# Second MoE layer on one core: raw weights given back earlier, converted weights stored later and in column parts, probability rows fetched one job earlier, and another order at the end

## The chip, the cores and the metric

The program runs on one NeuronCore of a Trainium2 chip. The metric is the device time of one execution in microseconds (us). TensorE is PE in the profile, VectorE is DVE, ScalarE is ACT, GpSimd is POOL; SyncE (SP) computes nothing here and issues the DMA transfers.

## The reference

Three layers follow one another on 2304 tokens of width 512, all in fp32: a causal decayed attention, a squared-ReLU layer with a hidden width of 2048, and a layer of four experts of hidden width 1024 that are weighted by probabilities and all added up.

```python
ret = scale * (q @ k.T) * Dmat;  x = ret @ v            # 4 batches, 8 heads, 576 x 64
h = x @ w_in;  g = max(h, 0) ** 2;  x = g @ w_out        # 512 -> 2048 -> 512
p = domain_probs / domain_probs.sum(-1)                  # 2304 x 4
for e in range(4):
    h = np.maximum(x @ w1[e], 0.0)                       # 512 -> 1024
    out += p[:, e:e+1] * (h @ w2[e])                     # 1024 -> 512
```

## The kernel before

**Precision.** PE multiplies in a rounded fp32 format. Each fp32 operand is therefore split into a high and a low part (`hi`, `lo`), and each product is three matmuls: hi·hi, hi·lo, lo·hi. The splitting is a copy on ACT (L130) and a subtraction on POOL (L131). A "matmul" below is one 128x128 weight tile against 512 columns; the usual step is six of them.

**Stages.** Attention takes the first 79 us of the span, the first layer (chunks c = 0 to 7 of its hidden width) runs to about 487 us, and the rest is the expert layer. That layer has 16 chunks, four to an expert, and passes over them twice: pass 1 (c = 8 to 23) serves the tokens of groups 0, 1 and 4, pass 2 (c = 24 to 39, from about 911 us) those of groups 2 and 3. Groups have 512 tokens, group 4 has 256.

**Seven products.** Two groups are treated together as a 2x2 block matrix, and its product with the 2x2 blocks of the weights is made by seven products instead of eight. For this the weights are needed as the four raw blocks (A11, A12, A21, A22; H11, H12, H21, H22) and as four sums of them (S1 to S4; for w2 t[0] to t[3]). In pass 1 the first multiplication of a chunk is `layer1_pair` (seven such products, ReLU and split in between), in pass 2 it is `first_layer`; the second multiplication in pass 1 is plain (`layer2_2`, which adds into `oacc`), in pass 2 it is `second_layer`, also seven products, which gathers into the four `sums`. `outputs` adds the last chunk, multiplies by a scale (`back`), and writes.

**Weights.** In pass 1 raw weights come by DMA into three buffers (`wraw`, `load_piece`); a chunk's w1 and w2 have two pieces each, and `load_piece()` asks for the next one as soon as one can be freed. `split_w1` and `split_w2` make the eight blocks (sums on DVE, L167 and L199; copies on ACT; subtractions on POOL), and `keep` stores the result to DRAM (L210), so that pass 2 only has to `fetch` it (L223). These functions are generators: every `yield` is a step, and `tick(pace)` runs `pace` steps of the queue `work` behind each group of matmuls. In pass 1 a chunk has 36 ticks at pace 3; conversion and storing want 26 steps of a chunk.

**Order.** Every engine works through its instructions in program order, and SP does so with the DMAs: an instruction that waits holds up all that stand behind it on its engine. So where a step stands in `work` decides what it can hold up. The list `jobs` gives the order of the multiplications; the last are pair(22), pair(23), group 4 of chunk 22, group 4 of chunk 23, and pair(24) of pass 2; the second multiplication of a job follows one job later. `probabilities()` (L771) broadcasts four rows of probabilities to all partitions, into the memory of the accumulators of groups 0 and 1; `first_layer` multiplies with them after its ReLU (L802).

**Pass 2.** Each of the seven products of chunk c is followed by one of the seven steps of `second_layer(c-1)` (L875 matmuls; sums on DVE, L885). Operands of that layer need further differences on POOL (L805), split again; four of these are put off into `later`. The first product of a chunk, A11, is copied from its bank by ACT (L811), and the fourth, A12, is accumulated in the same bank.

Of the kernel before, what the change touches and what calls it, by code (L numbers as in the profile page):

```python
# [28 lines left out]
BC = 256  # L29
# [4 lines left out]
def tile_kernel(ctx, tc, qT, kT, kn, vn, v4d, mask, qdec, kdec, wd, w, probs, probs2, out, outT):  # L34
# [104 lines left out]
    def split_w1(c):  # L139

        hi = wp.tile([128, 8 * BC], F32R, name="w1hi")
        lo = wp.tile([128, 8 * BC], F32R, name="w1lo")
        blk = [slice(BC * i, BC * (i + 1)) for i in range(8)]
        if c < NW1:

            w1s[c] = [t[:, :W1C].rearrange("p (f k m) -> p f k m", f=FT, k=KT) for t in (hi, lo)]
            for i in range(4):
                r = wraw.pop((c, i))
                yield from from_f64(r, hi[:, blk[i]], lo[:, blk[i]])
                load_piece()  # L150
# [12 lines left out]
        for i in (A11, S2, S3, A12, S1, A22, S4, A21):  # L163
            for _ in range(2 if todo else 0):
                yield
                o, x, y, op = todo.pop(0)
                v.tensor_tensor(out=o, in0=x, in1=y, op=op)  # L167
            yield
            split(src[i], hi[:, blk[i]], lo[:, blk[i]])
        load_piece()  # L170
        load_piece()

    def split_w2(c):

# [10 lines left out]
            return  # L185
        r = wraw.pop((c, 2)), wraw.pop((c, 3))
        a = [r[i // 2][:, BC * (i % 2) : BC * (i % 2 + 1)] for i in range(4)]
        for i in range(4):
            yield
            split(a[i], hi[:, blk[i]], lo[:, blk[i]])  # L190
        v = nc.vector
        t = [cvp.tile([128, BC], F32, name=n, bufs=2) for n in ("cv_m", "cv_d", "cv_m", "cv_d")]
        todo = [
            (t[0], a[H21], a[H22], ALU.add), (t[1], t[0], a[H11], ALU.subtract), (t[2], a[H21], a[H11], ALU.subtract),
            (t[3], a[H12], t[1], ALU.subtract),
        ]
        for i, (o, x, y, op) in enumerate(todo):
            yield
            v.tensor_tensor(out=o, in0=x, in1=y, op=op)  # L199
            yield  # L200
            split(o, hi[:, blk[4 + i]], lo[:, blk[4 + i]])
        load_piece()
        load_piece()

    def keep(f, c):

        yield
        for i, t in enumerate(w1t[c] if f is split_w1 else w2t[c]):
            d = dram.tile([128, 8 * BC], F32, name=f"kept{int(f is split_w2)}_{c}_{i}")
            nc.sync.dma_start(out=d, in_=f32(t))  # L210
            kept[f, c, i] = d

    def fetch(f, c):

        names = ("w2hi", "w2lo") if f is split_w2 else ("w1hi", "w1lo")
        parts = ((0, 3), (4, 8))
        if f is split_w2:
            parts = ((0, 1), (2, 8)) if c < NW - 1 else ((0, 4),)
        t = [wp.tile([128, 8 * BC], F32R, name=n) for n in names]
        for a, b in parts:  # L220
            for i in range(2):
                p = slice(BC * a, BC * b)
                nc.sync.dma_start(out=f32(t[i][:, p]), in_=kept[f, c - NW2, i][:, p])  # L223
# [19 lines left out]


    order = [(f, c) for c in range(NW) for f in (split_w1, split_w2)]
    splits = {}
    free = {(f, c) for f in (split_w1, split_w2) for c in range(2)}

    held = {(split_w2, NW1), (split_w1, NW1 + 1)}
# [1 line left out]
    def queue_weights(*place):  # L251
        free.update(place)
        while order and order[0] in free and order[0] not in held:
            f, c = order.pop(0)
            if c >= NW1 + NW2:
                fetch(f, c)
                continue
            splits[f, c] = f(c)
            work.append(splits[f, c])
            if c >= NW1:  # L260
                work.append(keep(f, c))


    def attention(a):
# [230 lines left out]
    with tc.manual_schedule():  # L495
# [428 lines left out]
        def outputs(c):  # L924
# [8 lines left out]
                nc.scalar.activation(out=t, in_=t, func=ACTF.Copy, scale=0.5)  # L933
                back.append(t)
            e1, e2, e3, e4 = totals()
            for a, b, op in ((e2, e1, ALU.add), (e3, e2, ALU.subtract), (e4, e3, ALU.subtract)):
                for d in range(2):
                    x, y = (a, b) if op == ALU.add else (b, a)
                    nc.gpsimd.tensor_tensor(out=a[d], in0=x[d], in1=y[d], op=op)
            for e, half, g, xs in (  # L940
                (e1, 0, 1, ("11", "21")), (e2, 0, 0, ("12", "22")), (e3, 1, 0, ("12", "22")), (e4, 1, 1, ("11", "21"))
            ):
# [43 lines left out]
        for i, job in enumerate(jobs):  # L986
# [2 lines left out]
            if c < NW1 + NW2:  # L989
                drain(splits[split_w1, c])  # L990

            pace[0] = 4 if i < 3 else 3 if c in (p, q) else 4 if c == z else 3 if c >= NW1 else 2
            if job == (NW1, (0, 1)):

                drain(sa[2])
# [38 lines left out]
            while i > 2 and len(pend) > 1:  # L1034
# [2 lines left out]
                layer2(done)  # L1037
                if j == last[done[0]]:
                    queue_weights((split_w2, done[0] + 2))
            if job == (z, (4,)):  # L1040
                probabilities()
            if job == (p, (3,)):
                rescale(0, s)
# [2 lines left out]
        sums += [yp.tile([128, 4, GT], F32, name=f"sums{i}", tag=f"acc{i}") for i in (2, 3)]  # L1046
        for c in range(NW1 + NW2 + 1, NW):
            f, t = first_layer(c), second_layer(c - 1)
            for _ in f:
                if later:  # L1050
                    later.pop(0)()
                next(t)
            queue_weights((split_w1, c + 2), (split_w2, c + 1))
        outputs(NW - 1)

# [71 lines left out]
```

## Time and profile before

| | |
|---|---|
| median of 3 runs | 1243.87 us (1243.79 to 1249.62) |
| the profiled execution's own time | 1243.94 us |
| its span, first to last instruction | 1242.0 us |
| PE busy | 1202.4 us (97%) |
| DVE busy | 897.5 us (72%) |
| POOL busy | 681.6 us (55%) |
| ACT busy | 435.3 us (35%) |
| mean granted PE clock | 0.994 |
| pass 1 of the expert layer | from about 480 to 911 us |
| pass 2 | from about 911 us to the end |

A busy PE does not say that nothing can be gained: what counts is where PE stands still, and what ended each such pause. A matmul that begins after a pause is shown with the idle time and the instruction that released it. After a long pause the granted clock can be below 1.00, and the matmuls behind it then take longer.

### The profile page before, as it was taken

Reading aid. Unit: us, or ns where it says so; the run is one execution under the profiler, and the core shown is the slowest. Engines: PE = TensorE matmul, PEld = TensorE weight load, DVE = VectorE, ACT = ScalarE, POOL = GpSimd, SP = SyncE. Lnnn points to the kernel's source line nnn. Section 1 sums busy time; section 2 is a strip of 40 time slices with the busy share of each in tenths; the row PEclk is TensorE's granted clock in tenths of the full one; section 3 lists DMA queues with packets and bytes.
Section 4 is the critical chain, followed back from the end, with each engine's and each line's share of the span. In section 5 each row is a group of like instructions: output and inputs, shape, how many; then the busy total and the mean of one; then the engine's idle time right before and its main releaser. Section 6 shows DMA issues by size and latency. Waiting matters only on the chain.

```text
span 1242.0 us, 18075 instructions
## 1 busy us (share of the span) xinstructions
PE 1202.4 (97%) x6470; PEld 1006.1 (81%) x6470; DVE 897.5 (72%) x1522; ACT 435.3 (35%) x1036; POOL 681.6 (55%) x695
## 2 busy tenths in 40 slices
PE   7999999999999999999999999999979999999997
PEld 6888888888888887778888878888768888888885
DVE  3777677777787688466777786767846877878777
ACT  4545433333333344533333433333402222222221
POOL 5646555545455435554553454533207777777776
PEclk9999999999999999999999999999989999999999
DMA  9921111111111002665455445555366465464551
GB/s 338 315 80 59 43 43 51 43 52 43 51 43 52 17 8 90 251 246 221 185 233 209 170 169 209 223 205 203 127 253 236 153 222 193 163 237 157 199 170 68
DMA packets 60989, 187.26 MB, mean 151 GB/s; under 512 B 7650, under 2 KB 12514, under 8 KB 52708
## 3 DMA queue, kind: packets, MB, share of 16 engines
q1 hardware_dynamic: 60388, 185.40, 40.9%
q8 instruction: 51, 0.84, 0.3%
q10 hardware_dynamic: 512, 0.70, 0.2%
q14 instruction: 38, 0.31, 0.1%
HBM read 114.23 MB, written 71.85 MB: 150 GB/s over the span
## 4 chain that ended last, share of the span: by engine, by line
PE 81%; DVE 9%; DMA 3%; ACT 2%; issue 2%; POOL 1%; SPq 0%; ACTq 0%; DVEq 0%; POOLq 0%
PE h L546 18%; PE o L741 14%; PE o L710 14%; PE h L792 11%; PE h L875 11%; PE h L580 10%; DMA wraw<-w 2%; DVE xl L669 1%; PE qk L347 1%; DVE y L637 1%; DMA k_n<-kn 1%; DMA rows<-rows 1%; PE xo L399 1%; DVE y L676 1%; DVE oacc L749 1%
## 5 line engine op out<-in xcount | busy, mean ns | idle before, releaser
L131 POOL TENSOR_TENSOR glo<-r,ghi 128x512 fp32r<-128x512 f32 (+1 forms) x80 | 96.9, 1212 | 153.6 <-ACT ghi L130 143.4
L546 PE MATMUL h<-xh,w1hi 128*128 128x512 f32 (+1 forms) x448 | 154.1, 344 | 0.8 <-DVE xl L434 0.8
L546 PE MATMUL h<-xl,w1hi 128*128 128x512 f32 (+1 forms) x448 | 154.0, 344 | 0.0
L546 PE MATMUL h<-xh,w1lo 128*128 128x512 f32 (+1 forms) x448 | 153.9, 344 | 0.0
L885 DVE TENSOR_TENSOR sums<-sums,h 128x512 f32<-128x512 f32 x202 | 128.5, 678 | 1.9 <-PE h L875 1.9
L741 PE MATMUL o<-w2hi,ghi 128*128 128x512 f32 x320 | 125.3, 392 | 3.1 <-DVE oacc L749 3.0
L741 PE MATMUL o<-w2hi,glo 128*128 128x512 f32 x320 | 125.0, 391 | 0.0
L741 PE MATMUL o<-w2lo,ghi 128*128 128x512 f32 x320 | 124.7, 390 | 0.0
L131 POOL TENSOR_TENSOR w2lo<-wraw,w2hi 128x256 fp32r<-128x256 f32 x64 | 52.2, 844 | 128.0 <-ACT w2hi L130 128.0
L710 PE MATMUL o<-glo,w2hi 128*128 128x512 f32 (+1 forms) x320 | 118.1, 369 | 1.0 <-POOL glo L131 1.0
L710 PE MATMUL o<-ghi,w2hi 128*128 128x512 f32 (+1 forms) x320 | 117.8, 368 | 0.0
L710 PE MATMUL o<-ghi,w2lo 128*128 128x512 f32 (+1 forms) x320 | 117.7, 368 | 0.0
L749 DVE SCALAR_TENSOR_TENSOR oacc<-o,pr,oacc 128x512 f32<-128x512 f32 x150 | 108.7, 743 | 5.8 <-PE o L741 5.7
L551 DVE TENSOR_TENSOR r<-r 128x512 f32<-128x512 f32 (+1 forms) x80 | 62.3, 779 | 65.5 <-ACT r L550 65.2
L580 PE MATMUL h<-xh,w1hi 128*128 128x512 f32 x224 | 88.6, 396 | 7.6 <-ACT r L593 3.9
L792 PE MATMUL h<-xh,w1hi 128*128 128x512 f32 x224 | 88.8, 397 | 6.9 <-DVE spare_xh L799 6.9
L546 PEld LDWEIGHTS h<-xh,w1hi 128*128 128x128 f32 x448 | 84.9, 189 | 11.7 <-DVE xl L434 0.9
L546 PEld LDWEIGHTS h<-xl,w1hi 128*128 128x128 f32 x448 | 84.8, 189 | 10.5
L546 PEld LDWEIGHTS h<-xh,w1lo 128*128 128x128 f32 x448 | 84.8, 189 | 10.1
L718 DVE TENSOR_TENSOR y<-o,y 128x512 f32<-128x512 f32 (+1 forms) x140 | 86.2, 628 | 3.8 <-PE o L710 3.6
L580 PE MATMUL h<-xl,w1hi 128*128 128x512 f32 x224 | 87.9, 393 | 0.0
L580 PE MATMUL h<-xh,w1lo 128*128 128x512 f32 x224 | 87.7, 392 | 0.0
(162 smaller groups left out, 2904.2 us busy)
## 6 DMA issues: line engine op xcount, KB each, us to landing
wraw<-wd SPq DMA_DIRECT2D x64, 256.0 KB, 2.7
wraw<-w SPq DMA_DIRECT2D x64, 256.0 KB, 3.1
kept<-w1hi SPq DMA_DIRECT2D x16, 1024.0 KB, 5.2
kept<-w1lo SPq DMA_DIRECT2D x16, 1024.0 KB, 7.2
kept<-w2hi SPq DMA_DIRECT2D x16, 1024.0 KB, 5.8
kept<-w2lo SPq DMA_DIRECT2D x16, 1024.0 KB, 7.3
w2hi<-kept SPq DMA_DIRECT2D x15, 768.0 KB, 5.0
w2lo<-kept SPq DMA_DIRECT2D x15, 768.0 KB, 6.1
```

The lines of the kernel that those rows point to most:

```text
L131: nc.gpsimd.tensor_tensor(out=lo, in0=src, in1=f32(hi), op=ALU.subtract)
L347: nc.tensor.matmul(qk[:, j, w : w + m], k_t[p, o : o + C], q_t[p, o : o + m], start=True, stop=True, skip_group_check=True,)
L546: nc.tensor.matmul(h, wk(a, f, k), group(x, g, k), start=(n == 0), stop=(n == 3 * KT - 1))
L551: nc.vector.tensor_tensor(out=r, in0=r, in1=r, op=ALU.mult)
L580: nc.tensor.matmul(o, a[:, i, k, :], slot(x, j)[:, k, :], start=(first and n == 0), stop=(n == 5), skip_group_check=True,)
L710: nc.tensor.matmul(o, a[:, f, 128 * m : 128 * m + 128], x[:, f, :], start=(n == 0), stop=(n == 3 * FT - 1))
L718: nc.vector.tensor_tensor(out=y, in0=o, in1=y, op=ALU.add)
L741: nc.tensor.matmul(o, a[:, f, 128 * m : 128 * m + 128], x[:, f, :], start=(n == 0), stop=(n == 3 * FT - 1))
L749: nc.vector.scalar_tensor_tensor(out=acc, in0=o, scalar=pr[:, tt, e : e + 1], in1=acc, op0=ALU.mult, op1=ALU.add)
L792: nc.tensor.matmul(o, a[:, i, k, :], slot(x, j)[:, k, :], start=(first and n == 0), stop=(n == 5), skip_group_check=True,)
L875: nc.tensor.matmul(b, a[:, BC * i + 128 * d : BC * i + 128 * d + 128], o[x][:, y, :], start=(first and n == 0), stop=(n == 2), skip_group_ ...
L885: v.tensor_tensor(out=e, in0=e, in1=b, op=op)
```

## The change

1. `split_w1` asks for the next raw pieces behind A12 and behind A21. `split_w2` works on one raw piece after the other: H11, H21, then three sums, then asks for a piece; H12, H22, the fourth sum, asks for the other; the four splits of the sums come last.
2. `keep` stores only the columns that pass 2 fetches (seven of eight blocks; of the last w2 the four raw ones), in two parts per tile, one step each, and only once the next conversion has been queued (`stores`).
3. The last chunk's w2 (c = 23) is split without the sums, which nothing uses.
4. In the two chunks in which a group is rescaled (`scaled`: c = 12 and 16) the pace is 2 instead of 3.
5. `probabilities()` is called at the job (22, (4,)) instead of (23, (4,)).
6. At the end the second layer's steps of c = 38 stand only behind every second product of c = 39; the other four follow its last product. The sum e2 + e1 moves from POOL in `outputs` to DVE between those four.

```diff
@@ split_w1
             split(src[i], hi[:, blk[i]], lo[:, blk[i]])
-        load_piece()
-        load_piece()
+            if i in (A12, A21):
+                load_piece()
@@ split_w2
-        for i in range(4):
-            yield
-            split(a[i], hi[:, blk[i]], lo[:, blk[i]])
...
-        for i, (o, x, y, op) in enumerate(todo):
-            yield
-            v.tensor_tensor(out=o, in0=x, in1=y, op=op)
-            yield
-            split(o, hi[:, blk[4 + i]], lo[:, blk[4 + i]])
-        load_piece()
-        load_piece()
+        whole = c < NW1 + NW2 - 1
+        for piece in ((H11, H21), (H12, H22)):
+            for i in piece:
+                yield
+                split(a[i], hi[:, blk[i]], lo[:, blk[i]])
+            for _ in range((3 if piece[0] == H11 else 1) if whole else 0):
+                yield
+                o, x, y, op = todo.pop(0)
+                v.tensor_tensor(out=o, in0=x, in1=y, op=op)
+            load_piece()
+        for i in range(4 if whole else 0):
+            yield
+            split(t[i], hi[:, blk[4 + i]], lo[:, blk[4 + i]])
+
+    def needed(f, c):
+        if f is split_w1:
+            return (0, 3), (4, 8)
+        return ((0, 1), (2, 8)) if c % NW2 != NW1 - 1 else ((0, 4),)
@@ keep
-        yield
         for i, t in enumerate(w1t[c] if f is split_w1 else w2t[c]):
-            d = dram.tile([128, 8 * BC], F32, name=f"kept{int(f is split_w2)}_{c}_{i}")
-            nc.sync.dma_start(out=d, in_=f32(t))
-            kept[f, c, i] = d
+            kept[f, c, i] = d = dram.tile([128, 8 * BC], F32, name=f"kept{int(f is split_w2)}_{c}_{i}")
+            for a, b in needed(f, c):
+                yield
+                p = slice(BC * a, BC * b)
+                nc.sync.dma_start(out=d[:, p], in_=f32(t[:, p]))
@@ queue_weights
+                work.extend(stores); stores.clear()   # before a fetch
...
             work.append(splits[f, c])
+            work.extend(stores)
+            stores.clear()
             if c >= NW1:
-                work.append(keep(f, c))
+                stores.append(keep(f, c))
@@ jobs
-            pace[0] = 4 if i < 3 else 3 if c in (p, q) else 4 if c == z else 3 if c >= NW1 else 2
+            pace[0] = 4 if i < 3 else 3 if c in (p, q) else 4 if c == z else 3 if c >= NW1 and c not in scaled else 2
...
-            if job == (z, (4,)):
+            if job == (a, (4,)):
                 probabilities()
@@ pass 2, and outputs
-            for _ in f:
+            for i, _ in enumerate(f):
                 if later:
                     later.pop(0)()
-                next(t)
+                if c < NW - 1 or i % 2:
+                    next(t)
+            if c == NW - 1:
+                for i in range(4):
+                    next(t)
+                    if i == 2:
+                        ...  # e2 = e1 + e2 on DVE, two instructions
-            for a, b, op in ((e2, e1, ALU.add), (e3, e2, ALU.subtract), (e4, e3, ALU.subtract)):
+            for a, b in ((e3, e2), (e4, e3)):
```

On DVE, where the first pair of pass 1 (c = 8) makes its first two sums (`r`, `cv_tp`), there stood before two sums of the conversion of w1 right ahead of them (`wraw` is raw weights, L167 sums for w1, L199 for w2):

```order
L199 TENSOR_TENSOR cv_m<-wraw 128x256
L199 TENSOR_TENSOR cv_d<-cv_m,wraw 128x256
L199 TENSOR_TENSOR cv_m<-wraw 128x256
L199 TENSOR_TENSOR cv_d<-wraw,cv_d 128x256
L167 TENSOR_TENSOR cv_m<-wraw 128x256
L167 TENSOR_TENSOR cv_d<-cv_m,wraw 128x256
L587 TENSOR_TENSOR r<-h,r 128x512
L587 TENSOR_TENSOR cv_tp<-h,r 128x512
```

And of the change, at the same pair (L598 is the former L587, L202 the former L199):

```order
L167 TENSOR_TENSOR cv_m<-wraw 128x256
L167 TENSOR_TENSOR cv_d<-cv_m,wraw 128x256
L167 TENSOR_TENSOR cv_m<-wraw 128x256
L167 TENSOR_TENSOR cv_d<-wraw,cv_d 128x256
L202 TENSOR_TENSOR cv_m<-wraw 128x256
L202 TENSOR_TENSOR cv_d<-cv_m,wraw 128x256
L202 TENSOR_TENSOR cv_m<-wraw 128x256
L202 TENSOR_TENSOR cv_d<-wraw,cv_d 128x256
L598 TENSOR_TENSOR r<-h,r 128x512
L598 TENSOR_TENSOR cv_tp<-h,r 128x512
```

The four sums of w1 stand ahead of those of w2 as before, but no sum of the next w1 stands any longer between w2's sums and the pair's.

On SP, at the turn from pass 1 to pass 2, before (`out<-oacc` are results, `w2hi<-kept` and the like fetch converted weights, `rows` are the probabilities):

```order
L754 DMA out<-oacc_5284 128x512 x4
L754 DMA out<-oacc_5348 128x512 x4
L223 DMA w2hi<-kept_8_0_5254 128x256
L223 DMA w2lo<-kept_8_1_5256 128x256
L223 DMA w2hi<-kept_8_0_5254 128x1536
L223 DMA w2lo<-kept_8_1_5256 128x1536
L223 DMA w1hi<-kept_9_0_5328 128x768
L223 DMA w1lo<-kept_9_1_5330 128x768
L223 DMA w1hi<-kept_9_0_5328 128x1024
L223 DMA w1lo<-kept_9_1_5330 128x1024
L771 DMA rows_9137<-rows 128x1024 x2
L771 DMA rows_9140<-rows 128x1024 x2
```

And of the change, at the same place:

```order
L765 DMA out<-oacc_5278 128x512 x4
L765 DMA out<-oacc_5336 128x512 x4
L782 DMA rows_9127<-rows 128x1024 x2
L782 DMA rows_9130<-rows 128x1024 x2
L230 DMA w2hi<-kept_8_0_5334 128x256
L230 DMA w2lo<-kept_8_1_5346 128x256
L230 DMA w2hi<-kept_8_0_5334 128x1536
L230 DMA w2lo<-kept_8_1_5346 128x1536
L230 DMA w1hi<-kept_9_0_5479 128x768
L230 DMA w1lo<-kept_9_1_5490 128x768
L230 DMA w1hi<-kept_9_0_5479 128x1024
L230 DMA w1lo<-kept_9_1_5490 128x1024
```

The four rows now stand ahead of the eight fetches instead of behind them.

On PE, the end of the last chunk before (L792 first layer of c = 39, L875 second layer of c = 38):

```order
L875 MATMUL h<-ghi,w2hi 128x512 x2
L875 MATMUL h<-ghi,w2lo 128x512
L875 MATMUL h<-ghi,w2hi 128x512 x2
L875 MATMUL h<-ghi,w2lo 128x512
L792 MATMUL h<-xh_80,w1hi 128x512
L792 MATMUL h<-xl_83,w1hi 128x512
L792 MATMUL h<-xh_80,w1lo 128x512
L792 MATMUL h<-xh_80,w1hi 128x512
L792 MATMUL h<-xl_83,w1hi 128x512
L792 MATMUL h<-xh_80,w1lo 128x512
L875 MATMUL h<-glo,w2hi 128x512 x2
```

And of the change (L803 first layer of c = 39, L886 second layer of c = 38):

```order
L803 MATMUL h<-xl_83,w1hi 128x512
L803 MATMUL h<-xh_80,w1lo 128x512
L886 MATMUL h<-ghi,w2hi 128x512 x2
L886 MATMUL h<-ghi,w2lo 128x512
L886 MATMUL h<-ghi,w2hi 128x512 x2
L886 MATMUL h<-ghi,w2lo 128x512
L886 MATMUL h<-glo,w2hi 128x512 x2
L886 MATMUL h<-glo,w2lo 128x512
L886 MATMUL h<-glo,w2hi 128x512 x2
L886 MATMUL h<-glo,w2lo 128x512
```

Before, one step of the second layer followed each first-layer product up to the end; now the first layer's products are done first and four steps of the second layer close the chunk.

On ACT nothing changes there; of the change, in c = 39, the copy of A11 stands behind the copy of `spare_xh` that the operand `t1` of c = 38 needs:

```order
L130 CAST glo<-wraw 128x512
L130 CAST ghi<-spare_xl_9194 128x512
L130 CAST glo<-spare_xh_9193 128x512
L822 COPY r<-h 128x512
L130 CAST ghi<-spare_xl_9194 128x512
```

Before, the same five stood in this order (with L811 for L822).

## Rows read from the trace of the kernel before

**Rows 1.** The page: busy time of each engine, share of the span, instructions

```profile
PE 1202.4 (97%) x6470; PEld 1006.1 (81%) x6470; DVE 897.5 (72%) x1522; ACT 435.3 (35%) x1036; POOL 681.6 (55%) x695
```

**Rows 2.** Waits of PE, 500 to 1242 us: total, times, longest

```profile
PE h L792 <- DVE spare_xh L799: 6.9, 1, 6.9
PE h L580 <- ACT r L593: 3.2, 2, 2.1
PE o L741 <- DVE oacc L749: 3.0, 2, 1.6
PE h L580 <- DVE cv_tp L587: 2.9, 2, 1.9
PE h L949 <- ACT glo L130: 2.2, 1, 2.2
PE h L949 <- POOL glo L131: 0.9, 1, 0.9
```

**Rows 3.** Timeline of DVE, 508 to 517 us: start, length, instruction, [idle before <-releaser]

```profile
513.01 0.42 DVE L167 TENSOR_TENSOR cv_m<-wraw 128x256 f32<-128x256 f32 x1 [5.38 <-DMA wraw<-w]
```

**Rows 4.** Timeline of SP's queue, 500 to 516 us

```profile
504.90 0.42 SPq L210 DMA_DIRECT2D kept<-w1lo  x1
506.81 1.61 SPq L90 DMA_DIRECT2D wraw<-w  x2
```

**Rows 5.** The page's DMA issues: count, size, median us to landing

```profile
wraw<-w SPq DMA_DIRECT2D x64, 256.0 KB, 3.1
```

**Rows 6.** Windows: start:end, length, PE busy, ..., granted PEclk, DMA share, GB/s

```profile
524.00:548.00 24.00, 21.91 (x90) 17.64 (x89) 14.85 (x23) 8.11 (x22) 15.12 (x21) 0.93 0.75 287
...
920.00:940.00 20.00, 13.09 (x50) 10.54 (x50) 9.96 (x14) 3.59 (x6) 10.11 (x8) 0.83 0.70 262
```

**Rows 7.** Timeline of DVE, 874 to 899 us

```profile
879.76 0.97 DVE L199 TENSOR_TENSOR cv_m<-wraw 128x256 f32<-128x256 f32 x1
...
883.29 0.74 DVE L749 SCALAR_TENSOR_TENSOR oacc<-o,pr,oacc 128x512 f32<-128x512 f32 x1
```

**Rows 8.** Timeline of SP's queue, 900 to 927 us

```profile
901.71 5.78 SPq L754 DMA_DIRECT2D out<-oacc  x8
911.76 0.33 SPq L223 DMA_DIRECT2D w2hi<-kept  x1
...
915.92 3.62 SPq L771 DMA_DIRECT2D rows<-rows  x4
```

**Rows 9.** The instructions of line 771

```profile
DMA to landing us min/median/max: 9.7/9.9/10.2
```

**Rows 10.** Timeline of DVE, 912 to 930 us

```profile
916.07 0.69 DVE L799 TENSOR_TENSOR spare_xh<-h,r 128x512 f32<-128x512 f32 x1 [0.60 <-PE h L792]
925.68 0.69 DVE L802 SCALAR_TENSOR_TENSOR spare_xh<-h,rows 128x512 f32<-128x512 f32 x1 [8.92 <-DMA rows<-rows]
```

**Rows 11.** Timeline of POOL, 926 to 975 us: first L805 of c = 24 and of 25

```profile
931.36 1.74 POOL L805 TENSOR_TENSOR wraw<-spare_xl,spare_xh 128x512 f32<-128x512 f32 x1
...
951.80 1.80 POOL L805 TENSOR_TENSOR wraw<-spare_xl,spare_xh 128x512 f32<-128x512 f32 x1
```

**Rows 12.** Timeline of PE, 1199 to 1211 us: first matmul of A11 and of A12, c = 39

```profile
1201.45 0.39 PE L792 MATMUL h<-xh,w1hi 128*128 128x512 f32 x1
...
1209.69 0.50 PE L792 MATMUL h<-xh,w1hi 128*128 128x512 f32 x1
```

**Rows 13.** Timeline of ACT, 1200 to 1242 us

```profile
1208.53 0.62 ACT L130 CAST glo<-spare_xh 128x512 fp32r<-128x512 f32 x1 [3.37 <-POOL spare_xh L805]
1209.06 0.58 ACT L811 COPY r<-h 128x512 f32<-128x512 f32 x1
```

**Rows 14.** Timeline of DVE, 1218 to 1242 us

```profile
1226.97 0.69 DVE L954 TENSOR_TENSOR sums<-sums,h 128x512 f32<-128x512 f32 x1 [3.42 <-POOL sums L939]
...
1232.72 1.07 DVE L955 SCALAR_TENSOR_TENSOR sums<-sums,wraw 128x512 f32<-128x512 f32 x1
...
1238.40 0.69 DVE L955 SCALAR_TENSOR_TENSOR sums<-sums,wraw 128x512 f32<-128x512 f32 x1
```

More of the change, by code (lines that the diff above doesn't have):

```diff
@@ L196, in split_w2 @@
         ]
-        for i, (o, x, y, op) in enumerate(todo):
-            yield
-            v.tensor_tensor(out=o, in0=x, in1=y, op=op)
-            yield
-            split(o, hi[:, blk[4 + i]], lo[:, blk[4 + i]])
-        load_piece()
-        load_piece()
+        whole = c < NW1 + NW2 - 1
[9 more added lines that the diff above has]
+        for i in range(4 if whole else 0):
+            yield
+            split(t[i], hi[:, blk[4 + i]], lo[:, blk[4 + i]])
[3 more added lines that the diff above has]
+        return ((0, 1), (2, 8)) if c % NW2 != NW1 - 1 else ((0, 4),)
     def keep(f, c):
-        yield
         for i, t in enumerate(w1t[c] if f is split_w1 else w2t[c]):
-            d = dram.tile([128, 8 * BC], F32, name=f"kept{int(f is split_w2)}_{c}_{i}")
-            nc.sync.dma_start(out=d, in_=f32(t))
-            kept[f, c, i] = d
+            kept[f, c, i] = d = dram.tile([128, 8 * BC], F32, name=f"kept{int(f is split_w2)}_{c}_{i}")
[3 more added lines that the diff above has]
+                nc.sync.dma_start(out=d[:, p], in_=f32(t[:, p]))
     def fetch(f, c):
         names = ("w2hi", "w2lo") if f is split_w2 else ("w1hi", "w1lo")
-        parts = ((0, 3), (4, 8))
-        if f is split_w2:
-            parts = ((0, 1), (2, 8)) if c < NW - 1 else ((0, 4),)
         t = [wp.tile([128, 8 * BC], F32R, name=n) for n in names]
-        for a, b in parts:
+        for a, b in needed(f, c):
             for i in range(2):
@@ L245, in tile_kernel @@
     order = [(f, c) for c in range(NW) for f in (split_w1, split_w2)]
-    splits = {}
+    splits, stores = {}, []
     free = {(f, c) for f in (split_w1, split_w2) for c in range(2)}
@@ L259, in queue_weights @@
             work.append(splits[f, c])
+            work.extend(stores)
+            stores.clear()
             if c >= NW1:
-                work.append(keep(f, c))
+                stores.append(keep(f, c))
     def attention(a):
@@ L935, in outputs @@
             e1, e2, e3, e4 = totals()
-            for a, b, op in ((e2, e1, ALU.add), (e3, e2, ALU.subtract), (e4, e3, ALU.subtract)):
+            for a, b in ((e3, e2), (e4, e3)):
                 for d in range(2):
-                    x, y = (a, b) if op == ALU.add else (b, a)
-                    nc.gpsimd.tensor_tensor(out=a[d], in0=x[d], in1=y[d], op=op)
+                    nc.gpsimd.tensor_tensor(out=a[d], in0=b[d], in1=a[d], op=ALU.subtract)
             for e, half, g, xs in (
@@ L1048, in tile_kernel @@
             f, t = first_layer(c), second_layer(c - 1)
-            for _ in f:
+            for i, _ in enumerate(f):
                 if later:
                     later.pop(0)()
-                next(t)
+                if c < NW - 1 or i % 2:
[4 more added lines that the diff above has]
+                    if i == 2:
+                        e1, e2, _, _ = totals()
+                        for d in range(2):
+                            nc.vector.scalar_tensor_tensor(
+                                out=e2[d], in0=e1[d], scalar=1.0, in1=e2[d], op0=ALU.mult, op1=ALU.add
+                            )
             queue_weights((split_w1, c + 2), (split_w2, c + 1))
```

## The prediction

> **What bounds the kernel now.** The page's line for PE comes first: 97% of the span is busy [rows 1]. So no engine gives much by being faster; what there is to gain is PE's pauses, and what slow clock follows them. I then read PE's waits from 500 us on [rows 2]: six kinds, together 18.9 us. Each has an end in view, so I followed it on the engine that released it. The parts of the change touch all six.
>
> *First pass, 513 and 541 us.* DVE makes the conversion's sums in program order with the pair's own sums. At 513.01 it had idled 5.38 us for a raw piece [rows 3], while the pair's `r` and `cv_tp` stood behind it (first block of DVE's order in the change); PE waited 1.9 us for `cv_tp` [rows 2]. The raw piece was issued at 506.81, 1.9 us behind the start of a store of 1 MB [rows 4], and landed shortly before 513.0: some 6 us where the median is 3.1 [rows 5]. At 541 the same happens one chunk later: ACT copies a late conversion before `r` (2.1 us [rows 2]), and in 524 to 548 us PE ran at a granted clock of 0.93, of 21.9 busy us [rows 6].
>
> *About 730 us.* The other wait for ACT r and the other for cv_tp make 3.2 - 2.1 = 1.1 and 2.9 - 1.9 = 1.0 us [rows 2]. They lie in chunk 12, where the rescaling puts extra work on DVE and ACT beside conversions.
>
> *About 892 us.* DVE spends 879.76 to 883.29 on the four sums of the last w2 before it can add the first `oacc` [rows 7]; PE later waits twice for `oacc`, 3.0 us together [rows 2].
>
> *About 920 us.* PE's longest wait, 6.9 us [rows 2]: DVE's ReLU with the probabilities begins at 925.68 after 8.92 us of idling for the rows [rows 10]. SP issued them at 915.92 behind results and eight fetches [rows 8]; they take 9.7 us at best [rows 9]. Behind the wait PE's clock is 0.83 over 920 to 940 us, in 13.1 busy us [rows 6].
>
> *The end.* PE waits 2.2 + 0.9 us for the last operand [rows 2], and DVE then runs 16 instructions from 1226.97 to 1239.1 [rows 14].
>
> **The change part by part**
>
> (a) *513 us.* The order after has no sum of the next w1 between w2's sums and the pair's. The wait's 1.9 us and about 0.2 us around it go: 2.1. If raw pieces of w2 too were late, it would stay: 0 to 2.1.
>
> (b) *541 us.* The stores no longer go ahead of the very next raw load but a conversion later, an eighth smaller, and w2 gives its pieces back at its fifth and eighth step instead of after its last (twelve). The conversion of w1 can begin earlier by several steps, so ACT's copy of A11 has nothing late in front of it. Gain 2.1 us, and the clock's 0.07 x 21.9 = 1.5: 3.6 (0 to 3.6).
>
> (c) *730 us.* Fewer steps behind each group of matmuls at pace 2, and raw pieces in time: 2.1 us (0 to 2.1). What is not ticked is drained at the start of the next pair's job in one go; that is the place to be late next, and I leave 0.6 us for it and for the 61 additional store issues, which at some 0.4 us each [rows 4] are 26 us of SP's time over 430 us of pass 1, beside everything else.
>
> (d) *892 us.* Four sums less on DVE, 883.29 - 879.76 = 3.5 us [rows 7], against 3.0 us of PE's waits and some 0.4 us of smaller gaps ahead of them: 3.4 (2.5 to 3.8). ACT and POOL lose four instructions each, which nobody waited for.
>
> (e) *920 us.* SP's results end at 901.71 + 5.78 = 907.5 [rows 8]. The rows are issued next instead of at 915.92. At 9.7 us [rows 9] the first would be there at 917.2; the product whose ReLU needs it ends about 1.36 us behind the sum at 916.07 [rows 10], that is at 917.4 (a product takes (1209.69 - 1201.45) / 6 = 1.37 us [rows 12]). So the rows are in time, barely. Then the next sum of DVE, at 925.7 + 0.6 = 926.3 before, waits only for the next product, 917.4 + 1.4 = 918.8: 7.5 us earlier, and with it POOL, whose chain of differences begins there. The slow clock behind the pause has stretched POOL's first period to 951.80 - 931.36 = 20.4 us [rows 11] where fourteen products want 14 x 1.37 = 19.2: 1.2 more. Together 8.7. The bounds: 7.5, and PE's pause and clock, 6.9 + 0.17 x 13.1 = 9.1. The fetches were issued at 911.76, 4.3 us after the results [rows 8]: SP was then waiting for the buffer, not busy, and four rows (3.6 us of issuing [rows 8]) fit into just this gap. So fetches are hardly later. What bounds this from below is the sharing of the DMA engines: rows and fetches fly together in either order.
>
> (f) *The end.* In c = 39 six products lie between A11 and A12 (1201.45 to 1209.69 [rows 12]); now only one step of the second layer stands between them, four products, so PE is at A12 at 1201.45 + 4 x 1.37 = 1206.9. But A12 adds into the bank that ACT's copy of A11 reads, and that copy stands at 1209.06 behind a cast which waits for POOL until 1208.53 [rows 13], as before (ACT's order is unchanged). A new pause of 2.8 us, then, up to 1209.7. After it come ten products, A12 to H22, 13.7 us, and `outputs` begins at 1223.4 without waiting for its operand, which is six products old by then. Its first sum on DVE is due one product later, at about 1225.0 instead of 1226.97, and the 16 instructions take the same 12.1 us or less (no POOL beside them): gain 1.9. If the pause draws a slow clock behind it, 0.5; if the copy comes earlier and no pause arises, 1.9 + 1.4 = 3.3. I take 1.8.
>
> Of what POOL's sum costs on DVE: the two instructions read two SBUF inputs each, 0.69 us alone and 1.07 at worst beside POOL [rows 14], in a stretch where DVE waits for PE.
> The Trainium skill ("SBUF — State Buffer", section "SBUF: two separate sides") says that a VectorE instruction with two SBUF inputs and a GpSimd instruction that reads SBUF lock each other out for a whole instruction. The same form on DVE at 1232.72 took 1.07 us, though POOL's own instructions there lasted longer than the 0.4 us added; by the rule it would be some 2 us later, by the row 0.8, and both lie ahead of the last step's sums, so it moves nothing in (f).
>
> Sum: 2.1 + 3.6 + 2.1 + 3.4 + 8.7 + 1.8 = 21.7, less 0.6: **21.1 us**. The profiled execution took 1243.94 us, within 0.1 us of the median of 1243.87. Forecast: **1222.8 us**.
>
> **Rivals**
>
> *R1: raw pieces stay late.* Stores still stand ahead of raw loads in SP's queue, and seven eighths of the bytes remain. For it: the 6 us at 506.81 [rows 4]. Against: between them now lie steps of a conversion. Then (a) and (b) are lost, 5.7 us: 1228.5.
> The Trainium skill ("DMA: Bandwidth & Descriptors", section "Queues, rings and completion order") says that on each DMA engine descriptors are consumed in ring order. The landing behind a store agrees (6 us against 3.1); by it the later store helps only as far as it is drained when the load is issued, which is the condition of this rival.
>
> *R2: rows and fetches trade places.* The rows are in time, but w2(24) and w1(25) come several us late because the rows share the DMA engines with them. Against: the gap of 4.3 us in SP's issues. It halves (e): 1227.
>
> *R3: the end gives nothing.* The new pause at A12 draws the slow clock, (f) is 0: 1224.6.
>
> *R4, the other side: every pair waits.* After, DVE has eight conversion sums ahead of the pair's first two. If w2's second raw piece lands late in every chunk, all fourteen pairs from c = 9 to 22 get the pause of 513 us, 2.1 us, and with the 1.5 us of slow clock 3.6. That is 14 x 3.6 = 50 us at worst, 14 x 2.1 = 29 without the clock; less the 16.0 us of (c) to (f), 13 us slower: 1257. It decides from a landing later than the pair's own sums can bear, at 513 us from 512.9 - 2.1 = 510.8. Against: only two of sixteen pairs wait now.
>
> *R5: nothing happens*, because PE's pauses are only pushed to the next late thing (POOL paces pass 2): 1240 to 1246.
>
> **How the numbers follow.** Likeliest, all parts about as summed: 0.58, own range 1219 to 1226. R1: 0.13. R2: 0.11. R3: 0.07. More than summed (no new pause at the end, the smaller gaps of pass 1 gone too, up to 27 us): 0.05, 1217. R4: 0.03. R5: 0.03. The range reaches from 1217 to R1 and R2 with 1.5 us more: **1217 to 1230**; what is outside is R4, R5 and the heavier forms of R1 and R2, together about 0.15. A measurement can tell 0.5%, 6.2 us, from no change; so faster takes all but R4, R5 and a little: **0.94**, same **0.03**, slower **0.03**.
>
> **What would show it.** Right: no pause of PE over 1 us at the first two pairs, at chunk 12 and around 890 us; rows issued directly behind the results and DVE's first ReLU of pass 2 idle by less than 1 us; L816 on POOL (the former L805) starting with a period of 19.3 us; a pause of 2 to 3 us before A12 of c = 39 released by ACT's copy; DVE's last 16 instructions in 12 us from about 15 us before the end of the span. Wrong: SP's raw loads landing 6 us after their issue (R1, R4); PE waiting for `w2hi` or `w1hi` after 907 us (R2); clock under 0.95 in the last 30 us (R3); PE as long idle as before at new places (R5).

## The result and the profile after

The changed kernel takes 1227.16 us (median of 4 runs, 1225.97 to 1228.31) where before took 1243.98 us in the same comparison: a ratio of 0.985, 95% interval 0.982 to 0.988, or 17 us. The profiled execution is the longest of the four: 1228.31 us, span 1226.5 against 1242.0. The time lies inside the forecast range and 4.4 us above the forecast of 1222.8. What is to be learned is in those 4.4 us, and in terms that came out right for a wrong reason.

The waits of PE in the changed kernel, 490 to 1242 us (who waited for whom: total, times, longest), beside [rows 2]:

```profile
PE h L803 <- ACT r L822: 2.6, 1, 2.6
PE h L803 <- DMA w1hi<-kept: 1.6, 1, 1.6
PE h L591 <- ACT r L604: 1.4, 1, 1.4
PE h L886 <- DVE sums L896: 0.3, 1, 0.3
PE h L803 <- DMA w1lo<-kept: 0.2, 1, 0.2
```

Gone are the 6.9 us for the rows, the 3.0 us for `oacc`, both waits for `cv_tp` and both for the last operand. Three waits are new or in a new place: for w1 of c = 25 at 914 us, for ACT's copy at 694 us, and the forecast one for ACT's copy of A11 in c = 39 (L822, the former L811). Windows of the changed kernel around the turn of the passes (length, PE busy, DVE, ACT and POOL behind it, granted clock, DMA share, GB/s), beside [rows 6]:

```profile
902.00:920.00 18.00, 16.13 (x71) 12.73 (x70) 9.82 (x14) 3.56 (x6) 8.49 (x6) 1.00 0.96 364
920.00:940.00 20.00, 20.00 (x90) 16.57 (x89) 15.19 (x23) 4.25 (x7) 13.25 (x11) 1.00 0.58 211
```

The slow clock of 920 to 940 us is gone; but in the window before it the DMA engines are now 96% busy. SP's queue there, 899 to 910 us, and DVE's first ReLU of pass 2 (the former 8.92 us of idling [rows 10]):

```profile
900.35 3.38 SPq L782 DMA_DIRECT2D rows<-rows  x4
...
906.30 0.43 SPq L230 DMA_DIRECT2D w1hi<-kept  x1
```

```profile
907.27 0.69 DVE L813 SCALAR_TENSOR_TENSOR spare_xh<-h,rows 128x512 f32<-128x512 f32 x1 [0.67 <-PE h L803]
```

The rows come in time: DVE waits for PE, not for a transfer. PE pays for it later, when it comes to A11 of c = 25:

```profile
915.66 0.50 PE L803 MATMUL h<-xh,w1hi 128*128 128x512 f32 x1 [1.63 <-DMA w1hi<-kept]
```

That w1 was issued at 906.30 and could be used at 915.62, over 9 us later. At the end, ACT's copy, PE, and DVE's queue of the changed kernel (three timelines), beside [rows 12 to 14]:

```profile
1191.70 0.62 ACT L130 CAST glo<-spare_xh 128x512 fp32r<-128x512 f32 x1 [3.35 <-POOL spare_xh L816]
1192.22 0.58 ACT L822 COPY r<-h 128x512 f32<-128x512 f32 x1
```

```profile
1192.85 0.50 PE L803 MATMUL h<-xh,w1hi 128*128 128x512 f32 x1 [2.58 <-ACT r L822]
...
1195.24 0.63 PE L886 MATMUL h<-glo,w2lo 128*128 128x512 f32 x1
```

```profile
1198.88 0.69 DVE L810 TENSOR_TENSOR spare_xh<-h,spare_xh 128x512 f32<-128x512 f32 x1 [1.01 <-PE h L803]
...
1205.33 3.66 DVE L896 TENSOR_TENSOR sums<-sums,h 128x512 f32<-128x512 f32 x6
1208.92 1.28 DVE L1070 SCALAR_TENSOR_TENSOR sums<-sums 128x512 f32<-128x512 f32 x2
1210.12 1.27 DVE L896 TENSOR_TENSOR sums<-sums,h 128x512 f32<-128x512 f32 x2
1211.32 0.68 DVE L964 TENSOR_TENSOR sums<-sums,h 128x512 f32<-128x512 f32 x1
...
1222.48 0.69 DVE L965 SCALAR_TENSOR_TENSOR sums<-sums,wraw 128x512 f32<-128x512 f32 x1
```

The copy still stands behind the cast that waits for POOL, PE stands for 2.6 us, matmuls then take 0.63 instead of 0.39 us for a while, and from 1198.88 us on DVE is never idle again until its last sum: its queue, not PE, ends the kernel.

The accounts on PE, each pause with its restart and with the slow matmuls behind it:

| term | forecast gain | measured on PE |
|---|---|---|
| (a), (b): 513, 541 us | 5.7 | 6.3 |
| (c): 730 us, less new waits | 1.5 | 2.6 gone, 1.6 new at 694 us: 1.0 |
| (d): 892 us | 3.4 | 3.4 |
| (e): rows | 8.7 | 9.2 gone, 2.4 new at 914 us: 6.8 |
| (f): end | 1.8 | -1.3 (see below) |
| ahead of the change | 0 | -1.0 |
| sum | 21.1 | 15.2 (span: 15.5) |

The line "ahead of the change" is no clear effect of it: PE starts the last matmul ahead of the first pause of the first pair of pass 1 (c = 8) at 479.5 us before and at 480.5 after, but in the profiles of this study the point lies anywhere from 478.2 to 481.2 us.

### The profile page after: what moved, and what is told of

It reads as the page before. It is cut to its first block, busy times and chain, and to the rows that moved or that the text cites. A ratio compares the mean times of both kernels' runs of the same rounds, so it can differ in the third digit from the quotient of the medians.

```text
span 1226.5 us, 18174 instructions
## 1 busy us (share of the span) xinstructions
PE 1196.7 (98%) x6470; PEld 1003.8 (82%) x6470; DVE 904.1 (74%) x1520; ACT 434.8 (35%) x1032; POOL 682.0 (56%) x689
## 4 chain that ended last, share of the span: by engine, by line
PE 83%; DVE 8%; ACT 2%; DMA 2%; issue 2%; POOL 1%; SPq 0%; ACTq 0%; DVEq 0%; POOLq 0%
PE h L557 18%; PE o L752 15%; PE o L721 14%; PE h L803 11%; PE h L886 11%; PE h L591 11%; DVE xl L680 1%; PE qk L358 1%; DMA wraw<-w 1%; DMA k_n<-kn 1%; DMA w1lo<-kept 1%; PE xo L410 1%; DVE y L687 1%; DVE y L648 1%; ACT st L394 1%
## 5 line engine op out<-in xcount | busy, mean ns | idle before, releaser
L760 DVE SCALAR_TENSOR_TENSOR oacc<-o,pr,oacc 128x512 f32<-128x512 f32 x150 | 109.4, 744 | 19.3 <-PE o L752 18.9
L131 POOL TENSOR_TENSOR w1lo<-wraw,w1hi 128x256 fp32r<-128x256 f32 x64 | 50.0, 781 | 89.5 <-ACT w1hi L130 87.6
L803 PE MATMUL h<-xh,w1hi 128*128 128x512 f32 x224 | 88.6, 395 | 4.2 <-ACT r L822 2.6
L803 PE MATMUL h<-xh,w1lo 128*128 128x512 f32 x224 | 87.5, 391 | 0.2 <-DMA w1lo<-kept 0.2
L803 PE MATMUL h<-xl,w1hi 128*128 128x512 f32 x224 | 87.4, 390 | 0.0
```

The costliest lines, as they stand in the source:

```text
L131: nc.gpsimd.tensor_tensor(out=lo, in0=src, in1=f32(hi), op=ALU.subtract)
L760: nc.vector.scalar_tensor_tensor(out=acc, in0=o, scalar=pr[:, tt, e : e + 1], in1=acc, op0=ALU.mult, op1=ALU.add)
L803: nc.tensor.matmul(o, a[:, i, k, :], slot(x, j)[:, k, :], start=(first and n == 0), stop=(n == 5), skip_group_check=True,)
```

## The experiments

Medians differ by up to 2 us between comparisons, so each kernel is held against before as it ran on the same chip; the changed kernel's ratio is 0.9854. Where the total cannot tell, PE's pauses in the profile do.

**Undoing the end** (`x1_end_as_before`).

```diff
-                if c < NW - 1 or i % 2:
-                    next(t)
-            if c == NW - 1: ...      # four steps and e2 + e1 on DVE
+                next(t)              # and the three sums on POOL in outputs
```

> The change with its last part undone: the steps of the second layer again behind every product of c = 39, e2 + e1 again on POOL. Theory E (the new end loses: it brings A12 forward to a copy on ACT that does not move, 2.7 us of pause and 1.6 us of slow clock, and leaves DVE two sums more): the stretch from A12 of c = 39 to the end is 32.3 us as before instead of 33.7, so about 1.3 us faster than the changed kernel, and no pause at A12. Rival (the new end gains the 1.8 us that were forecast and the loss lies elsewhere): 1.8 us slower.

Measured: 1227.93 us, ratio 0.9861 (0.9841 to 0.9881). From POOL's last `wraw` difference (L816) to the end of the span it is 1226.1 - 1184.97 = 41.1 us, and 1226.5 - 1185.42 = 41.1 us with the new end. So the two ends are worth the same within what is measured; neither theory's number came. With the old end the wait for the last operand is back (2.2 + 0.8 us), and the slow clock lies on the last products instead (two windows of this run):

```profile
1185.00:1205.00 20.00, 18.63 (x82) 14.82 (x80) 15.44 (x24) 5.26 (x9) 16.62 (x13) 1.00 0.25 79
1205.00:1227.00 22.00, 14.20 (x48) 10.91 (x48) 12.81 (x19) 1.67 (x3) 9.60 (x7) 0.76 0.26 96
```

**The rows late again** (`x2_rows_late`).

```diff
-            if job == (a, (4,)):
+            if job == (z, (4,)):
                 probabilities()
```

> The change with the rows of probabilities fetched behind the eight fetches again. Theory R (the rows' place is worth what PE's longest wait and its slow clock showed, less the 2.4 us for which PE now waits for w1 of c = 25): 6 to 8 us slower than the changed kernel, and no wait of PE for w1. Rival (rows and fetches merely trade places): within 2 us, with the wait for w1 gone and one for the rows in its place.

Measured: 1233.81 us, ratio 0.9909 (0.9893 to 0.9925), 0.0055 or 7 us above the changed kernel. PE waits 6.8 us behind DVE for the rows and not at all for w1. Theory R holds. The price of the rows ahead is seen in the other direction too: here w1 is issued at 902.45 and lands 6.9 us later, at 909.3; in the changed kernel it lands at 915.6. This profile has the same 2.6 us pause at A12 of c = 39, but no slow clock behind it, and from L816 to the end it takes 1230.7 - 1191.39 = 39.3 us instead of 41.1.

**A11's copy ahead of the cast** (`x3_copy_first`).

```diff
-                if later:
+                if later and i < 6:
                     later.pop(0)()
```

> The change, with the operand t1 of the second layer asked for one product later, so that ACT's copy of A11 stands ahead of the cast that waits for POOL. Theory E: the pause at A12 of c = 39 (2.7 us) goes, the slow clock behind it (1.6 us), and the 0.17 us at A12 of each of the last eight chunks; up to 5 us faster, less what DVE's queue of sums at the end takes back, so 2 to 5. Rival (POOL's chain of differences sets the pace and the end, whatever ACT does first): the pause moves to the next thing that waits for POOL, within 1 us of the changed kernel.

Measured: 1220.75 us, ratio 0.9804 (0.9787 to 0.9821): 6 us faster than the changed kernel, the largest gain of a single edit over it. ACT's timeline in c = 39:

```profile
1183.48 0.62 ACT L130 CAST ghi<-spare_xl 128x512 fp32r<-128x512 f32 x1
1184.00 0.58 ACT L822 COPY r<-h 128x512 f32<-128x512 f32 x1
1187.48 0.62 ACT L130 CAST glo<-spare_xh 128x512 fp32r<-128x512 f32 x1 [2.90 <-POOL spare_xh L816]
```

The copy no longer waits 3 us. The pause at A12 and its slow clock are gone, and POOL's `wraw` difference comes back every (1181.18 - 933.91) / 13 = 19.02 us instead of (1185.42 - 934.94) / 13 = 19.27. So on POOL (1) 250.5 - 247.3 = 3.2 us are lost all along pass 2, near 0.25 in each of thirteen chunks, and (2) the stretch from the last L816 to the end falls from 41.1 to 37.6 us. The rival, POOL as the pacemaker by itself, is refuted.

PE shows little of (1): its pauses at A12 before c = 39 come in the last eight chunks alone, some 0.2 us each. DVE shows all of it. Its first sum of a chunk (`r`) needs the copy; DVE's waits for it from 935 to 1200 us, first of the changed kernel, then of this run:

```profile
DVE r L810 <- ACT r L822: 61.0, 14, 5.6
```

```profile
DVE r L810 <- ACT r L822: 1.6, 1, 1.6
```

So the late copy keeps DVE idle for some 4 us in every chunk; its sums then stand in a row, and POOL gets its next operands late.

**The steps first** (`x4_steps_first`).

```diff
-                if c < NW - 1 or i % 2:
+                if c < NW - 1 or i < 3:
```

> The change, but the three early steps of the second layer stand behind the first three products of c = 39 instead of every second one, so that A12 comes six products behind A11 again. Theory E: no pause at A12, no slow clock, 4.3 us off PE; the end is then set by DVE or by the last operand on POOL, so 3 to 4 us faster than the changed kernel. Rival (the end is bound by DVE's sums alone, which stay as many): within 1 us.

Measured: 1223.78 us, ratio 0.9833 (0.9812 to 0.9854), some 3 us faster, though the interval touches that of the changed kernel. No pause at A12; from L816 to the end 1225.9 - 1187.78 = 38.1 us, 3.0 less. Theory E's pause and clock are thus worth 3 us in this profile; its span hides it, because PE waited 2.9 us for w1 of c = 25 in it and ran at a granted clock of 0.76 from 915 to 922 us.

**Stores at once; loads late; both** (`x5_store_at_once`, `x6_load_late`, `x9_both_undone`).

```diff
-                stores.append(keep(f, c))
+                work.append(keep(f, c))          # x5, x9
...
-            if i in (A12, A21):
-                load_piece()
+        load_piece()                              # x6, x9: behind the last split,
+        load_piece()                              # w2 in its old order
```

> The change, but each conversion's stores stand in the work directly behind that conversion, as before; their parts, the places of the loads and w2's order stay. Theory S (the pauses of 513 and 541 us went because the stores went out of the way of the next raw load): both pauses come back, with the raw load landing some 6 us after its issue; 4 to 6 us slower than the changed kernel. Rival L (they went because w2 gives its raw pieces back earlier): within 1 us, no pause over 1 us between 500 and 560 us.

> The change, but split_w1 and split_w2 ask for the next raw pieces only after their last split, and w2 is split in its old order; stores stay late and in parts. Theory L: the pauses of 513 and 541 us come back, 4 to 6 us slower than the changed kernel. Rival S: within 1 us.

Measured: 1225.63 us, ratio 0.9824 (0.9806 to 0.9842), and 1227.76 us, 0.9853 (0.9838 to 0.9867). Neither shows a pause between 500 and 560 us. In each case the other half could have been enough, so the third run undid both.

> The change with both first-pass parts undone together: stores directly behind their conversion, and raw pieces asked for late with w2 in its old order; the stores' parts and smaller size stay. Theory T (either part alone is enough to keep raw loads clear of the first pairs, as the two runs that undid one of them showed no pause there): now the pauses of 513 and 541 us come back, 4 to 6 us on PE by 560 us; in the total up to 2.5 us less, because PE then comes to the fetched w1 of c = 25 later and waits less for it. Rival Q (the size and the parts of the stores did it): no pause over 1 us between 500 and 560 us, within 1 us of the changed kernel.

Measured: 1227.09 us, ratio 0.9853 (0.9839 to 0.9866), and again no pause there. So neither the stores' lateness nor the loads' places removed the pauses of 513 and 541 us. (The pairs of 513 and 541 us are those of c = 9 and 10, and the two orders of DVE under the change belong to c = 9, not 8, whose pair lies at 480 us.) What did remove them is seen on DVE in this run, 504 to 524 us:

```profile
506.12 0.96 DVE L200 TENSOR_TENSOR cv_m<-wraw 128x256 f32<-128x256 f32 x1
510.31 0.69 DVE L596 TENSOR_TENSOR r<-h,r 128x512 f32<-128x512 f32 x1 [3.23 <-PE h L589]
511.60 0.69 DVE L596 TENSOR_TENSOR cv_tp<-h,r 128x512 f32<-128x512 f32 x1 [0.60 <-PE h L589]
...
522.01 0.41 DVE L167 TENSOR_TENSOR cv_m<-wraw 128x256 f32<-128x256 f32 x1
```

The pair's `r` and `cv_tp` wait for PE alone, and the sum that stood ahead of them at 513.01 before [rows 3] comes at 522.01, behind the pair. At 541 us it is ACT's order: before, seven casts of the next w1 (537.13 to 540.60) stand directly ahead of the pair's copy; in this run the copy comes right behind w2's. ACT before, then in this run:

```profile
540.20 0.40 ACT L130 CAST w1hi<-wraw 128x256 fp32r<-128x256 f32 x1
540.50 0.57 ACT L593 COPY r<-h 128x512 f32<-128x512 f32 x1
```

```profile
535.70 0.41 ACT L130 CAST w2hi<-cv_d 128x256 fp32r<-128x256 f32 x1 [1.17 <-DVE cv_d L200]
536.01 0.58 ACT L602 COPY r<-h 128x512 f32<-128x512 f32 x1
```

The raw pieces are not early at all. Times from issue to landing of the raw loads from 500 to 560 us (least, median, most), first of the changed kernel, then of this run:

```profile
DMA to landing us min/median/max: 2.6/2.9/6.5
```

```profile
DMA to landing us min/median/max: 2.6/3.0/5.0
```

(Before, the view gives 2.6/3.0/3.2, but the piece that DVE waited for at 513 us, issued at 506.81, has no landing in that profile.) What both undone parts leave in place is that storing takes four steps of the work instead of one (and an eighth fewer bytes). Four steps make 32 instead of 26 of a chunk's 36, so the conversions run less far ahead. In the program's order this alone decides it for the pair of 513 us: written with the four parts of a store in one step and all else as in the change, DVE has the old order again:

```
L202 TENSOR_TENSOR cv_m<-wraw 128x256
L202 TENSOR_TENSOR cv_d<-wraw,cv_d 128x256
L167 TENSOR_TENSOR cv_m<-wraw 128x256
L167 TENSOR_TENSOR cv_d<-cv_m,wraw 128x256
L598 TENSOR_TENSOR r<-h,r 128x512
L598 TENSOR_TENSOR cv_tp<-h,r 128x512
```

That program was not run. So it is shown that late raw pieces do no harm once the next w1's sums and casts stand behind the pair; that the number of steps is what moved them, and so is worth the 6.3 us, is read from the order only.

**The last w2's sums back** (`x7_z_sums`).

```diff
-        whole = c < NW1 + NW2 - 1
+        whole = True
```

> The change, but the last w2 (c = 23) is again split with its four sums. Theory Z (the sums on DVE were what held up oacc around 892 us): PE waits for oacc again, 3.0 to 3.6 us slower than the changed kernel. Rival (after the other parts DVE is early enough there to bear them): within 1 us.

Measured: 1228.75 us, ratio 0.9856 (0.9841 to 0.9871), no difference from the changed kernel. But not for the rival's reason: the wait for `oacc` is back in full, and another is gone. PE's waits in this run:

```profile
PE o L752 <- DVE oacc L760: 3.0, 2, 1.6
PE h L803 <- ACT r L822: 2.6, 1, 2.6
PE h L591 <- ACT r L604: 1.3, 1, 1.3
PE h L886 <- DVE sums L896: 0.3, 1, 0.3
```

There is no wait for w1 here. PE starts A11 of c = 25 at 915.95, some 2 us later than the changed kernel stood ready for it (915.66 - 1.63 = 914.03), and finds it there; w1 was also issued and landed earlier in this run (905.48, 8.3 us to landing). So of the 3.4 us of (d) some 2.4 are given back 25 us later.

**Pace 3** (`x8_pace_3`).

```diff
-            pace[0] = ... 3 if c >= NW1 and c not in scaled else 2
+            pace[0] = ... 3 if c >= NW1 else 2
```

> The change with pace 3 in chunks 12 and 16 as before. Theory P (the lower pace keeps DVE's and ACT's backlog of conversions away from the pair behind the rescaling): the two pauses that lay at 727 and 731 us come back, 2 to 3 us slower than the changed kernel; the new pause at 694 us stays, since it lies ahead of chunk 16's ticks. Rival (they went with the earlier raw pieces): within 1 us, no pause between 700 and 740 us.

Measured: 1226.49 us, ratio 0.9841 (0.9826 to 0.9856), no difference. The pauses of 727 and 731 us stay away, as the rival has it; but the pause at 694 us goes, against theory P, and one of 1.9 us stands at 616 us, again for ACT's copy behind a conversion. The pace only moves that pause. That the earlier raw pieces removed the others is not shown: with pace 2 and late loads (`x6_load_late`, `x9_both_undone`) they stay away too, and no run has pace 3 and late loads together.

**One row ahead, and with the copy** (`x10_one_row_first`, `x11_copy_and_row`).

```diff
             if job == (a, (4,)):
-                probabilities()
+                probabilities(0)
+            if job == (z, (4,)):
+                probabilities(1, 2, 3)
```

> The change, but only the row of the first expert goes ahead of the eight fetches (0.5 MB instead of 2.1), the other three behind them. Theory R (rows and fetches share the DMA engines, so the rows ahead are what makes w1 of c = 25 late): the wait for w1 goes, 0.4 to 3 us, so some 2 us faster than the changed kernel, and the runs spread less than its 2.3 us. Rival (w1 is late because of when SP can issue it, or of the results ahead of it): the wait stays, within 0.5 us.

Measured: 1226.30 us, ratio 0.9844 (0.9829 to 0.9858). The wait for w1 is gone:

```profile
PE h L807 <- ACT r L826: 2.6, 1, 2.6
PE h L591 <- ACT r L604: 1.8, 1, 1.8
PE h L890 <- DVE sums L900: 0.4, 1, 0.4
```

So the rows ahead of it made w1 late. They did it in two ways, which this run does not separate: w1 is issued at 903.86 instead of 906.30, because SP has three rows less to issue before it, and it lands 7.6 instead of 9.3 us later. The first is the rival's reason, and the larger part. The total moved by about 1 us, within its uncertainty, and the spread stayed (1224.1 to 1227.02): less than forecast.

> The two together: ACT's copy of A11 ahead of the cast for t1, and one row ahead of the fetches. If the two are independent: 6 us for the first and what one row first gives alone (some 2 us), 1218 to 1220. If the copy's gain had part of its cause in w1 being early in that run: as the copy alone, about 1221.

Measured: 1218.59 us (1217.33 to 1219.84), ratio 0.9785 (0.9770 to 0.9799), as the first alternative has it. This is the best version found: 8 us faster than the changed kernel. The row's share in it is uncertain, since the intervals of this run and of the copy alone overlap.

**The copy's place in the kernel before** (`x12_before_copy_first`; the edit of the third experiment).

> The kernel before with one edit, ACT's copy of A11 ahead of the cast for t1. Theory C (in pass 2 the copy behind that cast ties PE to POOL's chain, 0.25 us in each of 14 chunks): the period of a chunk in pass 2 falls from 19.27 to 19.02 us, 3.2 to 3.6 us faster than before. Rival (POOL's chain sets the pace by itself, and only the changed end, with A12 closer to A11, gains from the copy): period 19.27, within 1 us of before.

Measured: 1242.28 us over 12 runs, ratio 0.9974 (0.9963 to 0.9986), 3.2 us faster than before. The period in pass 2 is (1198.19 - 950.64) / 13 = 19.04 us instead of 19.26 [rows 11 for the first two]. Theory C holds.

## Why the prediction was right, and where not

**(a) and (b)** were right in size (5.7 forecast, 6.3 measured) and wrong in the reason given for (b): "the stores no longer go ahead of the very next raw load ... and w2 gives its pieces back at its fifth and eighth step". Undoing both left the pauses away, and raw pieces land as late as 6.5 us after the change. The sentence under (a) on the order was the right one and holds for both, on DVE at 513 us and on ACT at 541; I had the additional store issues (126 against 64 in the profiles, 62 more and not 61) in view only as a cost on SP. R1's condition, late raw pieces behind stores, was met and did nothing. R4's was not: the piece that w2's sums wait for ahead of the pair of 513 us, issued at 502.73 in the changed kernel, landed 2.6 us later, well ahead of the 510.8 from which R4 decides. The rule put beside R1, from the Trainium skill ("DMA: Bandwidth & Descriptors", section "Queues, rings and completion order"), that each DMA engine takes descriptors in ring order, fits the late landings and was not what decided.

**(c)**: the pauses at 727 and 731 us went, but not by the pace, as the eighth experiment shows; by what stays open. They do not "lie in chunk 12" either: they are in the pair of c = 17, behind the rescaling of c = 16. The 0.6 us left for the drained conversions was too little: at 694 us (c = 16) ACT's copy of A11 stands behind conversions and the rescaling's magnitudes, 1.6 us.

**(d)** was right at its place (3.4 us) and worth nothing in the total that the seventh experiment can tell. The step that failed is the addition: a gain ahead of w1 of c = 25 is given back where PE waits for that transfer. It is shown for (d), some 2.4 of 3.4 us; that the gains of (a) to (c) end there too is inferred, since no run brings their pauses back. (The six waits that the prediction opens with add up to 19.1 us, not 18.9; nothing else is worked out from that.)

**(e)**: the mechanism was right, and the undone rows cost 7 us. Two of its terms were wrong. The rows do not take "9.7 us at best" once they are ahead of the fetches: they landed 3.9 to 5.8 us after their issue (L782 in the changed kernel), so the first was there at 904.3, 3 us before the ReLU of 907.27 and not "barely". And "So fetches are hardly later" was wrong: beside the run with late rows, w1 was issued 3.9 us later and took 2.4 us longer to land. Rows, results and fetches together fill the DMA engines (0.96 over 902 to 920 us), PE lost 2.4 us at w1, and R2 came true in part. In the profiles of kernels whose code there is the same, PE waited from nothing (`x5_store_at_once`, `x9_both_undone`) up to 2.9 us for it. That this makes the runs' spread is not shown: the run without the wait spread as much.

**(f)**: the new pause of 2.8 us was forecast and came (2.7 with the restart). Forecast were then 15.3 us from A12 to DVE's first sum of `outputs`; it took 1211.32 - 1192.85 = 18.5. Of the 3.2 us more, 1.6 are the slow clock, 0.5 a wait of PE for a bank that DVE had not yet emptied, and the rest, 1.1, DVE's lag behind PE: six sums in a row, the two that came from POOL, two more. "The 16 instructions" were counted, the queue ahead of them was not. So R3 came true in this profile. Against the old end the new one is worth about nothing in the runs.

**The rule on the shared port**, from the Trainium skill ("SBUF — State Buffer", section "SBUF: two separate sides"), says that whichever of the two begins first holds the port for its whole instruction, and the other waits. The prediction misread it: it charged each sum a whole POOL instruction, not the rest of one under way. The two moved sums began while POOL stood idle, and took 1.28 us for two. The trace does agree with the rule right behind them. POOL and DVE (two timelines of the changed kernel):

```profile
1211.32 1.29 POOL L949 TENSOR_TENSOR sums<-sums,sums 128x512 f32<-128x512 f32 x1
1212.56 1.74 POOL L949 TENSOR_TENSOR sums<-sums 128x512 f32<-128x512 f32 x1
```

```profile
1212.10 1.05 DVE L965 SCALAR_TENSOR_TENSOR sums<-sums,wraw 128x512 f32<-128x512 f32 x1
1213.07 0.68 DVE L964 TENSOR_TENSOR sums<-sums,h 128x512 f32<-128x512 f32 x1
1213.78 1.07 DVE L965 SCALAR_TENSOR_TENSOR sums<-sums,wraw 128x512 f32<-128x512 f32 x1
```

Each is stretched by what was left of the other's. L965, 0.69 us when it is alone, ends 0.55 us behind the end of the POOL instruction that it met (1213.15 against 1212.61, 1214.85 against 1214.30); the POOL instruction of 1212.56, some 1.29 us when nothing stands in its way, ends 1.15 us behind L965 (1214.30 against 1213.15). L964, which has one input in SBUF (`h` is in PSUM), keeps its 0.68 us in between. So the price is the rest of one instruction, 0.4 to 0.5 us here.

## What to carry to other kernels

When an in-order engine stalls on a late transfer, look at what stands behind the waiting instruction before making the transfer earlier: here the transfers stayed late, and moving a few small sums and casts behind the urgent ones was enough. Gains ahead of one common transfer don't add up: where PE already waits for a transfer, work saved in front of it is partly given back there, unless the transfer comes earlier as well. And a short copy that frees a PSUM bank should stand ahead of any instruction that waits for a slow engine: its price was near 0.25 us in each of thirteen chunks. The list of PE's waits never showed it; the distance of a repeated instruction divided by its count did, and so does the list of DVE's waits, where it stands first before the change as well (55.2 us in thirteen waits, 935 to 1200 us). An engine that is not the bottleneck can still set the pace of the chain.

## What was not expected of the hardware

The same pause of PE (2.6 us, same code, same place) was followed by matmuls at the lower of TensorE's two clock levels (1.2 instead of 2.4 GHz) in four of the eight profiles that have it, and not in the other four. Windows across the first microseconds behind it, of the changed kernel and of the run with late rows:

```profile
1192.00:1198.00 6.00, 5.15 (x16) 4.08 (x17) 4.45 (x7) 1.42 (x3) 4.88 (x4) 0.72 0.00 0
```

```profile
1198.00:1203.00 5.00, 4.20 (x18) 3.49 (x19) 4.21 (x7) 1.38 (x3) 3.92 (x4) 1.00 0.00 0
```

The stretch from the last L816 (or its equal in the runs) to the end is 40.7 to 41.1 us in the four profiles with the lower clock and 39.1 to 39.5 us in the others. A pause of that length therefore has two prices on PE here, 2.7 or 4.3 us, and neither is certain. Why one and not the other stays open.
